# The filter's second product on the whole array, first loads behind the positions, and another order at the end of the prologue

## The chip, the cores and the metric

The kernel runs on one core of a Trainium2 chip. The metric is device time in microseconds of one execution, as the median of several runs. A profile of one execution shows each engine's instructions, the waits between engines and the DMA traffic: TensorE (PE, with its weight loads as PEld), VectorE (DVE), ScalarE (ACT), GpSimd (POOL) and SyncE (SP), which here only issues transfers.

## The reference

A long convolution is followed by a feed-forward block. For x and v of 4 x 12544 x 128 (batch, positions S, channels):

```
h_filt = (max(pos_emb @ w1, 0) @ w2) * exp(-0.01 * pos)
y      = irfft(rfft(x * v, 2S) * rfft(h_filt, 2S))[:S]
a      = x * y
out    = max(a @ m1, a @ m2, a @ m3) @ m_out
```

pos_emb is 12544 x 64, w1 64 x 64, w2 64 x 128; m1 to m3 are 128 x 768 and m_out is 768 x 128. All is float32 (the weights of the feed-forward block arrive as 64-bit floats and are converted on the chip).

## The kernel before, in words

The Fourier transforms are matrix products. A position is split in two indices, and a transform has a first stage over one (a table f1, 2 x 90 columns) and a second stage over the other, with twiddles folded into tables of weights `wt`; 45 pairs of frequencies (NK = 45, index g or s) are worked on one after the other. The inverse has a third stage per pair and a last stage per tile of output.

The instruction order on every engine is written out by hand: the program's order is each queue's order, and the framework only adds the waits that data, buffers and pools call for. A tile of a new pool that lies where a closed pool lay waits for the readers of that whole pool.

**Start.** TensorE runs products on zeros (`warm_up`), the window is transposed (`window_back`, lines 279 to 287), and `mlp_in` / `mlp_out` make the hidden layer of the filter from the positions (pos_emb, loaded in eight pieces over the queues of SP and ScalarE, line 266, into the space of `specH`). Behind the pieces SP issues the first raw weights (`load_raw`, line 177) and the first six units (`u_load`, line 325; a unit is 4 groups of x and v).

**First stages.** 16 quads for the filter (64 channels, into `specH`) and 32 units of batch 0 (into `spec`), with the conversion of the weights on VectorE between.

**Pair loop** (lines 805 to 839). Step s runs, for each pair, on TensorE:

- `s_second(s)`: the filter's second stage, from `specH` and `wt`, into the PSUM tile gps (line 770), copied by ScalarE to G (line 775). Each frequency has two sums, of which one needs the negated real part: `s_minus` makes it on GpSimd (`minus`, line 758). Each pair so has 8 products of 128 columns.
- `g_second(s)`: the second stage of batch 0 (`ps<-spec,wt`, line 130), evens copied by ScalarE to eo (line 161), butterfly on VectorE (lines 155 and 156).
- `s_filter(s - 1)`: the product with w2 (line 788), 16 products of 64 rows by 64 columns of weights with 128 columns of w2x, on four quarters of the array at a time, into sps (one buffer); ScalarE copies it to ht (line 793), and GpSimd issues ht's store to hd (line 796) for the later batches.
- `g_third(0, s - 3)`: the inverse's third stage of an earlier pair (`ps<-ab,wt`, line 130), copied to zs (line 440) and stored to zd from ScalarE's queue (line 446).

ScalarE's `g_swap` (lines 409 and 410) and VectorE's `g_re`, `g_im` and `g_unfold` (lines 415 to 427) multiply spectrum and filter of pair s - 2 and leave `ab`, which the third stage reads. Late in the loop, units of batch 1 are loaded, multiplied (line 332) and turned (line 337, two units at a time).

**Drain.** Steps 45 to 47 finish the last pairs; eight first-stage products of batch 1 (`u_first`, line 139, units 0 to 3) lie between the last third stages. Then come two turns, six folds of the weights (`fold`: a transpose pt by `eye` on line 750, its copy w1t, and pl, line 130), and the first stages of units 4 and 5. `pro` is closed, and its space goes to the pools of the main stage.

**Main stage.** 128 tiles in 4 batches. `t_load(b, i)` issues, on SP, two loads of zt from zd (line 495) and four of xT (line 502); `t_sums` and `t_last` make the tile's input gt (sums even and zt, product yps, gt on VectorE, line 528); `up` (pa, pb) and `down` (ops) are the feed-forward block. The convolution of the next batch runs beside it in slots.

## Time and profile before

| what | value |
|---|---|
| median of 5 runs | 2398.15 us (2394.39 to 2399.14) |
| profiled execution | 2400.21 us, span 2398.4 us |
| TensorE busy | 2365.5 us (99%) |
| TensorE weight loads | 1516.2 us (63%) |
| VectorE busy | 1317.2 us (55%) |
| ScalarE busy | 1018.1 us (42%) |
| GpSimd busy | 702.5 us (29%) |
| chain that ended last | TensorE 95%, then DMA, VectorE, ScalarE, GpSimd and issue with 1% each |

A busy TensorE is one with products in flight. Each float32 product appears as two records. In the profile's rows, "128*64 128x128" is a product on 128 rows and 64 columns of the array with 128 columns streamed; two such, on the two column halves, run side by side. The idle time in brackets behind a row is that of the engine before the row, with what ended it. PEclk is the clock granted to TensorE, as a share of full speed.

### The profile page before, as it was taken

The numbers are of one execution on the slowest core, as the hardware profiler recorded it, in microseconds if no ns is written. First come the engines' busy times: TensorE is split into PE (matmuls) and PEld (weight loads), VectorE is DVE, ScalarE is ACT, GpSimd is POOL, SyncE is SP. The second block draws the span as 40 slices with busy tenths as digits, with TensorE's granted clock in tenths as the row PEclk, the third lists the DMA queues.
The fourth block names the chain that finished last, engine by engine and source line by source line (L and its number), as shares of the span: only waits on it lengthen the run. The fifth ranks groups of instructions, "written<-read, shape, count | busy, mean of one in ns | idle before, by whom it ended". The sixth has DMA issues, their size and how long they took to land.

```text
span 2398.4 us, 67636 instructions
## 1 busy us (share of the span) xinstructions
PE 2365.5 (99%) x27853; PEld 1516.2 (63%) x27853; DVE 1317.2 (55%) x2806; ACT 1018.1 (42%) x1978; POOL 702.5 (29%) x775
## 2 busy tenths in 40 slices
PE   8999999999999999999999999999999999999998
PEld 7989856656555556666656556666655555666665
DVE  5578844466666645446666644446666643333333
ACT  2688844444444434444444424444444432222222
POOL 2045423222323211101111111101111105666666
PEclk9999999999999999999999999999999999999999
DMA  7778968767777659977777859967777742222221
GB/s 164 186 222 268 281 160 172 171 188 208 210 209 212 185 128 192 170 179 211 216 210 211 220 125 180 189 156 218 211 209 211 215 138 55 69 57 55 66 64 21
DMA packets 532221, 408.43 MB, mean 170 GB/s; under 512 B 375859, under 2 KB 421996, under 8 KB 531913
## 3 DMA queue, kind: packets, MB, share of 16 engines
q1 hardware_dynamic: 422240, 315.25, 53.3%
q10 hardware_dynamic: 100233, 67.88, 9.6%
q0 software_dynamic: 9440, 20.98, 3.6%
q8 instruction: 219, 3.59, 0.6%
q14 instruction: 89, 0.73, 0.1%
HBM read 295.69 MB, written 84.67 MB: 159 GB/s over the span
## 4 chain that ended last, share of the span: by engine, by line
PE 95%; DMA 1%; DVE 1%; ACT 1%; issue 1%; POOL 1%; ACTq 0%; SPq 0%; POOLq 0%; DVEq 0%
PE pb L130 21%; PE pa L130 21%; PE ops L130 18%; PE ps L130 12%; PE ps L139 7%; PE ops L601 5%; PE yps L130 5%; PE gps L770 1%; PE sps L788 1%; PE pm L299 1%; PE pst L337 1%; PE pw L130 1%; DMA zd<-zs 0%; DMA ut<-in_vr_dram 0%; POOL out_dram L625 0%
## 5 line engine op out<-in xcount | busy, mean ns | idle before, releaser
L541 DVE TENSOR_TENSOR hid<-hid,pb 128x392 f32<-128x392 f32 x768 | 431.4, 562 | 725.7 <-PE pb L130 494.3
L538 ACT ACTIVATE hid<-pa 128x392 f32<-128x392 f32 x768 | 381.5, 497 | 788.0 <-PE pa L130 614.9
L130 PE MATMUL pb<-gt,w_sb 128*64 128x392 f32 x3072 | 641.4, 493 | 4.9 <-ACT hid L538 4.8
L130 PE MATMUL pa<-gt,w_sb 128*64 128x392 f32 x3072 | 642.9, 494 | 0.8 <-DVE gt L528 0.8
L130 PE MATMUL ops<-hid,wo_sb 128*64 128x392 f32 x2304 | 481.2, 492 | 0.0
L420 POOL TENSOR_TENSOR xt<-xt,xs 128x512 f32<-128x512 f32 x135 | 172.2, 1276 | 890.2 <-DVE xs L419 657.0
L130 PEld LDWEIGHTS pb<-gt,w_sb 128*64 128x64 f32 x3072 | 227.5, 137 | 286.4 <-issue 250.6
L130 PEld LDWEIGHTS ops<-hid,wo_sb 128*64 128x64 f32 x2304 | 173.5, 137 | 205.8 <-issue 162.1
L130 PEld LDWEIGHTS pa<-gt,w_sb 128*64 128x64 f32 x3072 | 202.8, 137 | 60.8 <-issue 34.1
L139 PEld LDWEIGHTS ps<-f,uT 98*64 98x64 f32 x4096 | 178.6, 137 | 47.4 <-issue 43.7
L130 PEld LDWEIGHTS ps<-ab,wt 128*64 128x64 f32 x2880 | 166.1, 137 | 48.0 <-issue 30.9
L130 PEld LDWEIGHTS ps<-spec,wt 128*64 128x64 f32 x2880 | 172.2, 137 | 37.7 <-issue 34.8
L130 PE MATMUL ps<-spec,wt 128*64 128x128 f32 x2880 | 193.9, 273 | 1.4 <-issue 1.4
L130 PE MATMUL ps<-ab,wt 128*64 128x128 f32 x2880 | 191.4, 274 | 0.0
L352 POOL COPY planes<-ut 128x784 uint16<-128x784 uint16 x90 | 75.9, 844 | 389.3 <-DVE ut L332 294.9
L139 PE MATMUL ps<-f,uT 98*64 98x90 f32 x4096 | 188.9, 241 | 0.4 <-ACT zs L440 0.3
L445 DVE TENSOR_TENSOR zs<-ps,z 128x256 f32<-128x256 f32 x270 | 102.0, 419 | 97.0 <-ACT z L443 94.9
L130 PEld LDWEIGHTS yps<-f4p,zt 90*64 90x64 f32 x3584 | 134.4, 138 | 25.9 <-issue 22.6
L409 ACT ACTIVATE xs<-xt 64x512 f32<-64x512 f32 x180 | 113.2, 629 | 73.8 <-DVE xt L156 59.9
L427 DVE TENSOR_TENSOR ab<-xt 128x256 f32<-128x256 f32 x360 | 136.0, 419 | 4.5
L130 PE MATMUL yps<-f4p,zt 90*64 90x49 f32 x3584 | 137.7, 222 | 0.4 <-DVE zt L511 0.4
L528 DVE TENSOR_TENSOR gt<-yps,xT 128x392 f32<-128x392 f32 x128 | 72.5, 566 | 111.8 <-PE yps L130 67.6
(114 smaller groups left out, 2545.3 us busy)
## 6 DMA issues: line engine op xcount, KB each, us to landing
wt<-wt_const SPq DMA_DIRECT2D x360, 256.0 KB, 4.6
ht<-hd SPq DMA_DIRECT2D x270, 256.0 KB, 4.5
zd<-zs ACTq DMA_DIRECT2D x180, 256.0 KB, 4.6
zt<-zd SPq DMA_DIRECT2D x256, 180.0 KB, 3.9
ut<-in_xr_dram SPq DMA_DIRECT2D x128, 196.0 KB, 3.5
ut<-in_vr_dram SPq DMA_DIRECT2D x128, 196.0 KB, 4.0
xT<-in_x_dram SPq DMA_DIRECT2D x512, 49.0 KB, 2.7
out_dram<-ot ACTq DMA_DIRECT2D x96, 196.0 KB, 4.0
```

The costliest lines, as they stand in the source:

```text
L130: nc.tensor.matmul(out[64 * h:64 * h + 64], lhsT[:, 64 * h:64 * h + 64], rhs, start=start, stop=stop, skip_group_check=True)
L139: nc.tensor.matmul(ps[64 * c:64 * c + 64, 256 * i + r * N1:256 * i + (r + 1) * N1], a[:, r, :], table[:, c * N1:(c + 1) * N1], start=(i % ...
L299: nc.tensor.matmul(ps[64 * h:64 * h + HH, 512 * r + q * FO:512 * r + (q + 1) * FO], posv[64 * h:64 * h + 64, P - 1 - 2 * (8 * i + q) - r, ...
L352: nc.gpsimd.tensor_copy(pl_[:, :, :, 0:NB], a[:].bitcast(U16).rearrange("p s (n h) -> p h s n", h=2))
L409: nc.scalar.mul(xs[0:64], xt[64:128], -1.0)
L420: (nc.gpsimd if apart else nc.vector).tensor_tensor(out=xt[:], in0=xt[:], in1=xs[:], op=ALU.add)
L427: nc.vector.tensor_tensor(out=ab[:, :, q, :], in0=y[:, :, 0, :], in1=y[:, :, 1, :], op=op)
L445: nc.vector.tensor_tensor(out=zs[:, a], in0=ps[:, 0:256], in1=z1[:], op=op)
L528: nc.vector.tensor_tensor(out=g[:].rearrange("d p (m a) -> d p m a", a=2), in0=y, in1=xT[:].rearrange("d p (m a) -> d p m a", a=2), op=ALU ...
L538: nc.scalar.activation(h[:], pa[:, 0:N], Relu)
L541: nc.vector.tensor_tensor(out=h[:], in0=h[:], in1=pb[:, 0:N], op=ALU.max)
L601: nc.tensor.matmul(ps[64 * c:64 * c + 64, 0:H2], w, rhs[:, H2 * c:H2 * c + H2], start=start, stop=True, skip_group_check=True)
```

## The change

Four things change in the part before the main stage, and one in the order of its loads.

1. `s_second` makes 4 products in place of 8: the products with the real and the imaginary part of `specH` go to the two halves of gps and are not added up there. `s_minus` and its tile go.
2. `s_filter` adds them up: `w2x` holds w2 twice, with signs (`signs`, four scaled copies on ScalarE in place of one), and 8 products on 128 rows and 64 columns, with 256 columns streamed, take the place of the 16 quarter-array products. ht is copied from contiguous PSUM.
3. `g_third(0, s - 3)` and the load of its weights stand first in a step, ahead of `s_second(s)`, not behind `s_filter(s - 1)`.
4. The first raw weights and the first six units are issued from ScalarE's queue, behind `window_back`, and the last three warm-up products go. In the drain only units 0 and 1 have their first-stage products between third stages. Those of units 2, 3 and 4 stand one by one between the folds, alternating copies on ScalarE and VectorE, and those of unit 5 behind them.
5. `t_load` issues the four loads of xT ahead of the two of zt.

```
-    w2x = pin.tile([P, D], FP32, name="w2x")
+    w2x = pin.tile([P, 2, D], FP32, name="w2x")
...
-    def w2_order():
-        nc.scalar.copy(w2x[:].rearrange("f (c g) -> f c g", c=GC),
-                       w2_in[:].rearrange("f (g c) -> f c g", c=GC))
+    def signs():
+        for sg, lo_, m in ((0, 0, 1.0), (0, FO, 1.0), (1, 0, -1.0), (1, FO, 1.0)):
+            nc.scalar.mul(w2x[lo_:lo_ + FO, sg].rearrange("f (c g) -> f c g", c=GC),
+                          w2_in[lo_:lo_ + FO].rearrange("f (g c) -> f c g", c=GC), m)
...
     def t_load(b, i):
+        xT = hp.tile([D, 4, NB], FP32, tag="xT", name="xT", bufs=2)
+        for c in range(GC):
+            nc.sync.dma_start(xT[c * NG:(c + 1) * NG], x[:, 4 * i:4 * i + 4, c, b, :])
+        xTs[b, i] = xT
         zt = hp.tile([N1, 2, 512], FP32, tag="zt", name="zt", bufs=2)
...
-        xT = hp.tile([D, 4, NB], FP32, tag="xT", name="xT", bufs=2)
-        for c in range(GC):
-            nc.sync.dma_start(xT[c * NG:(c + 1) * NG], x[:, 4 * i:4 * i + 4, c, b, :])
-        xTs[b, i] = xT
...
     window_back()
-    warm_up(3)
-    raws.append(load_raw(*jobs[0], nc.sync))
-    u_load(0, 0)
-    u_load(0, 1)
-    raws.append(load_raw(*jobs[1], nc.sync))
+    raws.append(load_raw(*jobs[0], nc.scalar))
+    u_load(0, 0, nc.scalar)
+    u_load(0, 1, nc.scalar)
+    raws.append(load_raw(*jobs[1], nc.scalar))
     for u in range(2, 6):
-        u_load(0, u)
+        u_load(0, u, nc.scalar)
...
     def s_second(g):
         ps = gps.tile([P, 512], FP32, tag="g", name="gps")
-        m = minus.pop(g)
         for k in range(2):
             for r in range(2):
-                for q in range(2):
-                    lhsT = m[:, k] if q and r == 0 else specH[:, 2 * g + k, r, :]
-                    nc.tensor.matmul(ps[64 * q:64 * q + 64, k * P:(k + 1) * P],
-                                     lhsT, wf[g][:, k, r, :],
-                                     start=(k == 0 and r == 0), stop=True,
-                                     skip_group_check=True)
+                nc.tensor.matmul(ps[64 * r:64 * r + 64, k * P:(k + 1) * P],
+                                 specH[:, 2 * g + k, r, :], wf[g][:, k, r, :],
+                                 start=(k == 0), stop=True, skip_group_check=True)
...
     def s_filter(g):
-        for ri in range(2):
+        for c in range(2):
             for k in range(2):
-                for q in range(2):
-                    for h in range(2):
-                        at = 512 * q + (2 * ri + k) * D
-                        nc.tensor.matmul(
-                            ps[64 * h:64 * h + 64, at:at + D],
-                            G[64 * q:64 * q + 64, k, ri, :], w2x[64 * q:64 * q + 64],
-                            start=(ri == 0 and k == 0), stop=True, skip_group_check=True)
+                for h in range(2):
+                    nc.tensor.matmul(
+                        ps[64 * h:64 * h + 64, (2 * c + k) * 2 * D:(2 * c + k + 1) * 2 * D],
+                        G[:, k, c], w2x[:].rearrange("p s d -> p (s d)"), start=(k == 0),
+                        stop=True, skip_group_check=True)
...
     for s in range(NK + 3):
+        if s >= 3:
+            ws[s - 3, 1] = wi.pop(s - 3)
+            g_third(0, s - 3)
+            if s < NK:
+                wi[s] = load_dir(s, 1)
         if s < NK:
             ws[s, 0] = wf[s]
             s_second(s)
-            if s + 1 < NK:
-                s_minus(s + 1)
...
-        if s >= 3:
-            ws[s - 3, 1] = wi.pop(s - 3)
-            g_third(0, s - 3)
-            if s < NK:
-                wi[s] = load_dir(s, 1)
...
-        if NK <= s < NK + 2:
-            for v in range(4):
-                u_first(2 * (s - NK) + v // 2, v % 2, nc.scalar.copy)
-    folded = [fold(0)]
+        if s == NK:
+            for u in (0, 1):
+                for h in range(2):
+                    u_first(u, h, nc.scalar.copy)
     u_turn(4)
     u_turn(5)
-    for f in range(1, NF):
+    folded = []
+    for f in range(NF):
         folded.append(fold(f))
-        folded.pop(0)()
+        u_first(2 + f // 2, f % 2)
+        if f:
+            folded.pop(0)()
     folded.pop()()
     nc.scalar.copy(lin[:], pl[:, 0:D])
-    for u in (4, 5):
-        for h in range(2):
-            u_first(u, h)
+    for h in range(2):
+        u_first(5, h)
     pro.close()
```

## Prediction, made before the change was run

> **What bounds the kernel now.** I cut the span into its stages and read TensorE's busy time in each. Columns: stretch, its length, then busy time and instruction count of each engine, granted clock, DMA share, GB/s.
>
> ```profile
> 0.00:18.88 18.88, 14.14 (x103) 8.31 (x104) 2.24 (x4) 2.45 (x5) 4.72 (x12) 1.00 0.91 196
> 18.88:40.54 21.66, 20.07 (x513) 19.95 (x513) 10.57 (x17) 0.00 (x0) 0.00 (x0) 0.92 0.58 124
> 121.38:302.22 180.84, 175.72 (x3537) 157.92 (x3537) 154.29 (x311) 151.19 (x268) 88.33 (x130) 1.00 0.86 258
> 302.22:326.06 23.84, 18.88 (x343) 15.65 (x343) 8.72 (x16) 11.45 (x26) 4.82 (x7) 0.94 0.46 126
> 326.06:2398.40 2072.34, 2058.16 (x21696) 1240.73 (x21696) 1088.29 (x2330) 800.38 (x1616) 593.97 (x607) 1.00 0.65 163
> ```
>
> The last 2072 us, which the change leaves alone but for the order of loads issued two tiles ahead, are TensorE at over 99%. So whatever the change saves or costs before 326 us moves the end by as much. Three places count: the start, the pair loop (121 to 302) and the drain (302 to 326).
>
> At the start, the chain of waits:
>
> ```profile
> 14.29 1.45 PE pw L130 x12
> 15.73 3.15 issue
> 18.88 20.09 PE pm L299 x512
> ```
>
> The 3.15 us are the wait for the last piece of the positions. The DMA view of 0 to 18.9 us says what else had moved by then:
>
> ```profile
> DMA packets 1781, 3.71 MB, mean 196 GB/s; under 512 B 991, under 2 KB 1048, under 8 KB 1780
> ```
>
> In the pair loop one iteration takes 3.93 us (the quarter-tile products of L788 start at 187.76 and 191.69). TensorE's timeline, then ScalarE's and VectorE's (start, length, engine and line, tiles, count, idle time before and what ended it):
>
> ```profile
> 187.76 1.10 PE L788 MATMUL sps<-w2x,G 64*64 64x128 f32 x32
> 188.80 1.09 PE L130 MATMUL ps<-ab,wt 128*64 128x128 f32 x16
> 189.80 0.32 PE L770 MATMUL gps<-wt,minus 128*64 128x128 f32 x1
> ```
>
> ```profile
> 186.30 1.01 ACT L793 COPY ht<-sps 128x1024 f32<-128x1024 f32 x1
> 187.21 0.59 ACT L440 COPY zs<-ps 128x512 f32<-128x512 f32 x1
> 187.83 0.41 ACTq L446 DMA_DIRECT2D zd<-zs  x1
> 188.28 0.37 ACT L775 COPY G<-gps 128x256 f32<-128x256 f32 x1 [0.48 <-PE ps L130]
> ```
>
> ```profile
> 187.34 0.69 DVE L415 TENSOR_TENSOR xt<-xt,ht 128x512 f32<-128x512 f32 x1 [0.18 <-ACT ht L793]
> 189.47 0.76 DVE L427 TENSOR_TENSOR ab<-xt 128x256 f32<-128x256 f32 x2
> ```
>
> ScalarE goes from piece to piece with its own DMA issue in the only gap: it is full. VectorE starts L415 the moment ht is copied. TensorE is nearly full too. It is two limits at once, not one.
>
> In the drain, the chain again:
>
> ```profile
> 316.14 0.28 PE pt L750
> 316.42 0.02 SPq L495
> ...
> 317.62 4.29 DMA zt<-zd
> ```
>
> The load of the main stage's first zt is let go by **the last fold's transpose (pt)**, not by the last store of zs: that store was issued at 312.58. The new pool's tiles lie where the transposes' weights lay, and wait for their last reader. TensorE idles 3.05 us before the first yps.
>
> **The change, part by part.**
>
> *First loads held back.* By 18.88 us 3.71 MB had moved. Positions are 6 x 320 + 2 x 352 KB, constants and w1, w2, window about 410 KB: 3.1 MB. So 0.6 MB were raw weights and units ahead of the positions' tail. At 3.71 MB in about 17 us (0.218 MB/us) they cost 2.75 us. Their place is not wholly the positions' (SP's half had landed before ScalarE's half), so I take **-2.3 us**, bounds -0.8 and -2.75. The warm-up products that go (1.45 us) lie in the wait. The 20 issues now stand in ScalarE's queue behind winr's copy at 14.6 us; each waits for a free DMA slot. Behind them are only the scaled copies of w2: four of at most the 0.41 us of the one copy before, done before ScalarE's next work at 42 us. The loads ended at 31 us on SP; by the same bandwidth they end about there again, and nothing reads them before 40 us. If they came 10 us later, that cover would be gone.
>
> The granted clock was 0.50 from about 19.3 to 23 us: 86 products in 19 to 23 us against 34 per us after it, 1.47 us lost. The new gap is about 2.3 us; gaps of 1.6 us (at 39 us) kept the clock, gaps of 3.05 and 3.15 lost it. Between these I take half: **-0.7 us**, bounds 0 and -1.47.
> [...]
>
> *Fill of the pair loop.* The negated copy on GpSimd goes, and with it the one long wait for it, 0.90 us at 130.2 us, and a like wait of 0.4 at 121.8, which I leave in as ScalarE's G must now be the first in that pool. But the first third stage now stands ahead of the fourth second stage and waits for its VectorE chain. From the loop's start: two second stages of each kind end at 2.6 us, the first filter product at 4.5, its ht is copied by 5.6, VectorE ends at 8.2, 0.4 for that like wait: 8.6 us. The third filter product stands 2.2 us behind: 132.2 us against 133.03. **-0.9 us**, bounds -1.5 and 0.
>
> *One iteration, TensorE.* Paired 128-column products follow each other every 0.109 us (two per product pair). The filter's second stage falls from 8 to 4 such slots: -0.44. The filter with w2 had 32 records, four at a time, in 8 slots (1.03 with the change of tile shape). Now it has 16 records of 256 columns, two at a time: 8 slots of about 0.216, from the warm-up's 128x256 rows (12 records in 1.45 us, tail included): 1.72. That is +0.85. The two changes of shape go: each showed 0.2 us from start to start in place of 0.109 and a first product of 0.32 for 0.27, about 0.145; -0.29. The wait for minus (189.80 in place of 189.73, and the second column half late by one slot from there) goes: -0.13. Sum: 3.93 + 0.85 - 0.44 - 0.29 - 0.13 = 3.92 us.
>
> *One iteration, ScalarE.* The same copies of the same sizes in the same cyclic order: 3.93.
>
> *One iteration, the chain.* Third stage g now stands right behind filter g+1, not one iteration later. From a third stage's start: third 0.87, second of the filter 0.44, g_second 0.87, filter 1.72 with 0.17 tail, then ht 1.01, VectorE 2.6 to the first half of ab (187.34 to about 189.9), three handovers 0.15, half of the wait for ab's second half 0.1: 7.93 us, over two iterations: 3.97. Before there were three iterations for it, so it never bound. In TensorE's queue everything stands behind that wait, so it is late as a whole. Three limits of 3.92, 3.93 and 3.97 leave no slack: I take 3.97, bounds 3.92 and 4.10.
>
> From the third filter product to the last but one lie 41 iterations, which took 166.1 us (133.03 to 299.17). After: 41 x 3.97 = 162.8; six unit products on VectorE (0.56 each, of which 0.2 is slack): 2.1; two double transposes at 1.25 each, half of before (the second no longer waits 1.0 to 1.5 us for the butterfly, as its buffer is another): 2.5; DMA 0.8. Sum 168.2: **+2.1 us**, bounds -1 and +7.
>
> *Drain.* The last third stage comes some 2.7 us earlier and its store too, but that store isn't what is waited for. The last transpose now stands behind five first-stage products and the other folds. From the last-but-one filter product's start: its ht is copied at 2.9 us, the last filter product runs 3.0 to 4.9, its ht is ready at 6.3 (zs and two xs first), VectorE's ab at 8.95, the last third ends at 9.8, both turns at 11.0, the first fold's first-stage product (after uT's copy) at 12.3; four rounds of 1.25 (transpose 0.26, product 0.62, pl 0.22 and a change of shape) and the last transpose, 0.33: 17.7 us, against 17.2 before (316.4 - 299.17): +0.5, bounds -1.5 and +1. Behind it SP now issues the four xT first, for which the row is
>
> ```profile
> 319.55 1.97 SPq L502 DMA_DIRECT2D xT<-in_x_dram  x4
> ```
>
> so zt starts 2.0 us later, of which some 0.5 may come back in a shorter landing (4.3 for the first, 3.6 for the second tile). Behind it the second tile's loads come no later than before, as the number of issues is the same; at a batch's end xT no longer queues behind zt's wait for zd, which nobody waits for. TensorE is out of work at 320 either way; its wait grows from 3 to about 5 us. The half clock that follows is there already (0.50 from 324 to 330); the yps now meet it whole, +0.3. **+2.3 us**, bounds -0.5 and +3.5.
>
> **Sum**: -2.3 - 0.7 - 0.9 + 2.1 + 2.3 = +0.5 us. The profiled execution took 2400.21 us (span 2398.4), 2.06 above the median of the runs, 2398.15. It would be 2400.7; the median 2398.7.
>
> **The rivals.**
>
> *The drain works as it reads.* If xT and zt were let go by the last third stage's store instead, zt would land before the first-stage products end; 3.05 us of idle time and some 2.5 us of half clock would go: -5.5 in place of +2.3, in all -7.3: 2390.9 us. Against it: the chain goes from pt to SP. For it: nothing but that the order of memory may change with the pool.
>
> *The chain binds the pair loop* (the other side). If third waits for both halves of ab, and VectorE's and ScalarE's jitter adds up, an iteration is 4.10: 41 x 0.13 = +5.3 more, 2404.0 us. It decides from 4.08 us an iteration on (+4.5, in all +5.0). For it: L415 already starts 0.03 us after ht. Against: the first and second half of ab are waited for apart in the drain.
>
> *The positions come no sooner* (the first part does nothing): if ScalarE's own half of the positions is slow by itself, its last piece lands as before: +3.0, 2401.7 us.
>
> **How the numbers follow.** The forecast, no change that can be told, has 0.47; the drain that works 0.15; the chain 0.23; the late positions 0.11; 0.04 is for what I don't see. 0.2% is 4.8 us, about what a measurement of this kernel can tell from no change. Below 2393.4: the working drain and 0.01 of the rest, 0.16. Above 2402.9: the chain and 0.03 of the rest, 0.26. Within: the forecast and the late positions, 0.58. The sum's bounds together (-3.0 to +7 in the loop and drain) give 2393 to 2406; taken down to the working drain's upper half, 2391.5 to 2406.
>
> **What would show it.** Right: pm starts at about 16.6 us; quarter-tile products are gone and an iteration is 3.95 to 4.0 us with third stage waiting for VectorE's L427; pt ends about 17.7 us behind the last-but-one filter product, the four xT stand between it and zt, and TensorE idles about 5 us before yps. Wrong: pm at 18.8; an iteration at 4.1 or at 3.8; zt issued before the last fold's transpose.

## The result: 2403.3 us in place of 2400.6, and the profile after

The changed kernel took 2403.34 us (median of 26 runs, 2398.60 to 2406.42), the kernel before, run beside it, 2400.64 us (median of 50, 2394.39 to 2403.59). The ratio is 1.0012, 95% interval 1.0006 to 1.0017: 2.8 us slower, within the 0.2% that the prediction called no change, 2.3 us above its sum. The interval does not reach 1: the loss is small, but it is one.

The first profile of the changed kernel is that of its fastest run (2398.60 us), while the one of before was near its median. Comparing the two would show a gain of 1.6 us that the runs do not have. So a second execution, `after_again` (2405.46 us in the profiled run), is read beside it. "Half clock" below is a stretch in which the granted clock was 0.50. Length of each stage in us:

| stage | before | after | after_again |
|---|---|---|---|
| start, until the positions' products (pm) | 18.88 | 17.86 | 17.66 |
| pm | 20.07 | 19.87 | 20.18 |
| first stages | 82.43 | 81.22 | 82.22 |
| loop's start to the third filter product | 11.64 | 10.55 | 10.54 |
| 41 iterations, to the last but one | 166.14 | 165.59 | 165.65 |
| from there to the first yps | 23.61 | 25.13 | 25.39 |
| from there to the first pa | 26.88 | 28.35 | 28.61 |
| first pa to the end | 2072.3 | 2073.4 | 2078.3 |

The stretches of the changed kernel, with the columns of the table before (stretch, its length, busy time and count of PE, PEld, DVE, ACT, POOL, granted clock, DMA share, GB/s):

```profile
0.00:17.86 17.86, 13.41 (x92) 7.90 (x92) 2.24 (x4) 2.04 (x4) 4.72 (x12) 0.99 0.87 194
17.86:37.73 19.87, 19.86 (x512) 19.71 (x512) 9.02 (x14) 1.74 (x4) 0.00 (x0) 0.92 0.59 146
118.95:298.13 179.18, 177.77 (x2490) 147.66 (x2490) 154.25 (x311) 152.16 (x269) 45.17 (x86) 1.00 0.86 263
298.13:323.45 25.32, 18.34 (x311) 15.20 (x311) 9.61 (x18) 10.12 (x23) 5.08 (x8) 0.89 0.38 100
323.45:2396.80 2073.35, 2058.76 (x21696) 1240.90 (x21696) 1088.78 (x2330) 801.42 (x1616) 596.03 (x607) 1.00 0.66 163
```

The loop is 1.7 us shorter than its 180.84 us before, and GpSimd has 45 us of work there in place of 88 (no negated copies). The drain is 1.5 us longer with less TensorE work in it.

**Start.** The DMA view of the first 17.86 us, then the chain of waits:

```profile
DMA packets 1257, 3.47 MB, mean 194 GB/s; under 512 B 477, under 2 KB 534, under 8 KB 1257
```

```profile
15.28 2.57 issue
17.86 19.88 PE pm L302 x512
```

3.47 MB in place of 3.71. Of the 0.6 MB that were to be kept out, some 0.37 (3.47 less the 3.1 of positions and constants) still went ahead of the positions' end: ScalarE's queue is free for them from 15 us on.

**Loop.** TensorE's timeline:

```profile
189.35 1.90 PE L777 MATMUL sps<-w2x,G 128*64 128x256 f32 x16
191.07 1.05 PE L130 MATMUL ps<-ab,wt 128*64 128x128 f32 x16
191.95 0.61 PE L763 MATMUL gps<-wt,specH 128*64 128x128 f32 x8
192.39 1.04 PE L130 MATMUL ps<-spec,wt 128*64 128x128 f32 x16
193.26 1.90 PE L777 MATMUL sps<-w2x,G 128*64 128x256 f32 x16
```

This iteration is 3.91 us, with products behind each other without a wait; most of the 41 take 3.91 or 3.96. VectorE's timeline for the same pair shows how close the chain is:

```profile
192.34 0.69 DVE L418 TENSOR_TENSOR xt<-xt,ht 128x512 f32<-128x512 f32 x1 [0.29 <-ACT ht L782]
...
194.39 0.76 DVE L430 TENSOR_TENSOR ab<-xt 128x256 f32<-128x256 f32 x2
```

The first of the two halves of ab is done at about 194.8; the third stage that reads it starts at 194.99. There are 0.2 us of slack, so here TensorE sets the pace and not the chain over VectorE.

**Drain.** SP's queue, then what SP, VectorE and TensorE waited for:

```profile
313.03 1.76 SPq L498 DMA_DIRECT2D xT<-in_x_dram  x4
314.96 1.95 SPq L502 DMA_DIRECT2D zt<-zd  x2
```

```profile
SPq L498 <- PE pt L753: 18.6, 1, 18.6
```

```profile
319.43 0.69 DVE L513 TENSOR_TENSOR even<-zt 90x512 f32<-90x512 f32 x1 [3.45 <-DMA zt<-zd]
320.22 0.46 PE L130 MATMUL yps<-f4p,even 90*64 90x49 f32 x4 [4.82 <-DMA xT<-in_x_dram]
```

The last fold's transpose lets go xT, and zt stands behind four xT. VectorE waits for zt to make `even`, and the product yps reads `even`; the row of yps names xT, which is only what landed last before it. TensorE is idle for 4.82 us (5.08 in `after_again`) in place of 3.05.

### The profile page after: what moved, and what is told of

Same layout as the page of the kernel before. It is cut to its first block, busy times and chain, and to the rows that moved or that the text cites. A ratio compares the mean times of both kernels' runs of the same rounds, so it can differ in the third digit from the quotient of the medians.

```text
span 2396.8 us, 65298 instructions
## 1 busy us (share of the span) xinstructions
PE 2366.8 (99%) x26761; PEld 1505.1 (63%) x26761; DVE 1318.6 (55%) x2808; ACT 1020.2 (43%) x1979; POOL 661.1 (28%) x730
## 3 DMA queue, kind: packets, MB, share of 16 engines
q10 hardware_dynamic: 106953, 71.08, 10.2%
## 4 chain that ended last, share of the span: by engine, by line
PE 96%; DMA 1%; issue 1%; POOL 1%; ACT 1%; SPq 0%; DVE 0%; ACTq 0%; POOLq 0%; DVEq 0%
PE pb L130 21%; PE pa L130 21%; PE ops L130 18%; PE ps L130 13%; PE ps L139 8%; PE ops L604 5%; PE yps L130 5%; PE sps L777 3%; PE pm L302 1%; PE gps L763 1%; PE pst L340 1%; DMA specH<-in_pos_emb_dram 1%; POOL out_dram L628 0%; DMA hd<-ht 0%; ACT ht L782 0%
## 5 line engine op out<-in xcount | busy, mean ns | idle before, releaser
L130 PEld LDWEIGHTS ops<-hid,wo_sb 128*64 128x64 f32 x2304 | 173.5, 137 | 205.8 <-issue 164.5
L130 PEld LDWEIGHTS ps<-spec,wt 128*64 128x64 f32 x2880 | 167.9, 137 | 39.1 <-issue 34.5
L418 DVE TENSOR_TENSOR xt<-xt,ht 128x512 f32<-128x512 f32 x180 | 126.6, 703 | 15.3 <-ACT ht L782 15.0
```

Source lines behind the costliest of these rows:

```text
L130: nc.tensor.matmul(out[64 * h:64 * h + 64], lhsT[:, 64 * h:64 * h + 64], rhs, start=start, stop=stop, skip_group_check=True)
L418: nc.vector.tensor_tensor(out=xt[:], in0=xt[:], in1=hts[g][:, 0], op=ALU.mult)
```

## Experiments

All ratios are to the kernel before, run on the same chip beside each. The rows come from several chips, so ratios are to be compared and not medians; times "by the ratios" below are a difference of ratios times 2400 us.

| kernel | median us | ratio | 95% interval |
|---|---|---|---|
| first loads alone (loads_only) | 2401.86 | 1.0002 | 0.9994 to 1.0011 |
| whole-array filter alone (filter_only) | 2396.44 | 0.9980 | 0.9971 to 0.9989 |
| + third stage first (filter_third_first2) | 2396.24 | 0.9984 | 0.9976 to 0.9993 |
| + the new drain (filter_third_drain) | 2400.36 | 0.9995 | 0.9986 to 1.0004 |
| + first loads (after_zt_first2) | 2401.84 | 1.0004 | 0.9995 to 1.0013 |
| + xT ahead of zt = the change | 2403.34 | 1.0012 | 1.0006 to 1.0017 |
| the change again (after_again) | 2406.82 | 1.0022 | 1.0013 to 1.0031 |
| everything but the filter (order_only) | 2413.99 | 1.0054 | 1.0040 to 1.0067 |
| the change, two waits filled (after_warm2) | 2401.51 | 1.0004 | 0.9996 to 1.0013 |

From filter_only to the change each row adds one part. Neighbours' intervals overlap, so no single step is shown by the runs alone; the ends, 0.9980 and 1.0012, are clearly apart. From end to end the ratios lose 7.7 us. The profiles say where the steps lie.

### after_again: the changed kernel once more

No edit.

> The changed kernel as it is, profiled a second time, as its one profile had a span 1.6 us below that of the kernel before while its median lies 2.8 us above. Theory A (clock): TensorE's half clock comes in windows of 3.4 us whose place varies; the longer wait ahead of the first yps (4.8 us against 3.05) makes one window more fall on busy work in most executions. Then this profile shows the same length of the pair loop within 1 us and a longer stretch at half clock in the start or the drain, and a span of 2399 to 2404. Theory B (loop): the pair loop itself varies, its third stage waiting for VectorE more often; then 41 iterations take 168 us or more in place of 165.6. Time 2.5 to 3 us above before.

2406.82 us, higher than the first set. Up to the first pa it is 1.2 us ahead of before; behind it, 6.0 us are lost, in part to four waits for loads of weights (2.7 us in all, the longest 1.7 at 1924.8) and to a stretch at half clock of 6.8 us from 1980.5, behind the wait at the last batch's end, which is 2.64 us in before and 3.33 us here. In fourteen profiles this last part took 2072.3 to 2078.3 us: 2074.0 on average in the ten with zt issued ahead of xT, 2076.4 in the four with xT first. Theory A, one more stretch at half clock in the start or the drain, is not what this profile shows: the extra stretch lies at the last batch's end, and the loop is the same to 0.1 us.

### loads_only, filter_only, order_only: the parts alone

loads_only:
```
-    warm_up(3)
-    raws.append(load_raw(*jobs[0], nc.sync))
+    raws.append(load_raw(*jobs[0], nc.scalar))
...
-        u_load(0, u)
+        u_load(0, u, nc.scalar)
```


> Of the change only the first loads behind window_back and the three warm-up products less. Forecast's account: the first product of the positions at 17.9 us (as in the changed kernel's profile) and not 18.9, and the time 1 to 3 us below before. Rival (positions no sooner, or clock and TensorE's earlier start cost what the loads give): within 0.5 us of before.

No change, as its rival had it. pm starts 1.1 us sooner (17.81), but now TensorE waits on without warm-up products, half clock lies over 6.8 us from 15.3 on, and pm takes 20.42 us.

filter_only (parts 1 and 2 of the change; loop order, drain, loads as before):
```
-                for q in range(2):
-                    lhsT = m[:, k] if q and r == 0 else specH[:, 2 * g + k, r, :]
...
+                nc.tensor.matmul(ps[64 * r:64 * r + 64, k * P:(k + 1) * P],
+                                 specH[:, 2 * g + k, r, :], wf[g][:, k, r, :],
...
+                        G[:, k, c], w2x[:].rearrange("p s d -> p (s d)"), start=(k == 0),
```


> Of the change only the filter's second stage in 4 products and the product with w2 on the whole array; the third stage stays behind the filter's product, the drain and the loads stay as before. Forecast's account: an iteration is bound by ScalarE at 3.93 and by TensorE at 3.92, the 0.13 us waits for minus are gone, so 41 iterations take 163 to 167 us against 166.1, and the time is -2 to +1 us of before, as the recovery at 3.80 after a disturbance is lost. Rival (the quarter tiles were worth more): 168 us or more and +2 to +5 us.

0.2% faster, more than the 2 us that were expected at most. The third filter product comes 8.77 us after the loop's start in place of 11.64 (1.3 us of this are two waits ahead of products that read the negated copies, 0.42 and 0.90 us; the profile names `minus` for the longer one); the 41 iterations take 165.35 us (-0.8), the drain 0.7 us less: 4.4 us in all, against 4.8 by the runs. (The 41 iterations vary by about 1 us: in loads_only, whose loop is that of before, they took 167.23 us against 166.14.)

order_only (third stage first, the new drain, xT first; filter and loads as before):
```
     for s in range(NK + 3):
+        if s >= 3:
+            ws[s - 3, 1] = wi.pop(s - 3)
+            g_third(0, s - 3)
```


> Of the change only the order: third stage first in a step, first-stage products between the folds, xT ahead of zt; quarter-array filter and early loads as before. Forecast's account: the drain costs 2 us (fold's last transpose as late as before, zt 2 us behind it, TensorE idle some 5 us ahead of yps), and the loop gains or loses under 2 us, so +1 to +4 us. Rival (the order is what helps): the main stage's first pa starts earlier behind the last-but-one filter product than the 26.9 us of before, and the time is below before.

13 us slower, which neither account had. The 41 iterations take 171.70 us. What TensorE's third stage waits for in the loop, here and then in the changed kernel (us in total, times, longest):

```profile
PE ps L130 <- DVE ab L427: 7.9, 18, 1.3
```

```profile
PE ps L130 <- DVE ab L430: 1.0, 2, 0.6
```

The longest wait of each row still lies ahead of the third filter product. With the quarter-array filter TensorE comes to the third stage before ab is there, every second iteration, though its own products take no longer. ScalarE's timeline of order_only shows why ht, and so ab, is late:

```profile
200.13 0.37 ACT L161 COPY eo<-ps 128x256 f32<-128x256 f32 x1 [0.35 <-PE ps L130]
201.80 1.01 ACT L793 COPY ht<-sps 128x1024 f32<-128x1024 f32 x1
```

The filter product ended at 201.11, but ScalarE copies eo and then xs twice (1.67 us) first, and can begin only when the second stage of batch 0 is done. Under the 1.03 us of the quarter-array product these copies do not fit, and ht comes 0.69 us late. In the changed kernel they lie under the whole-array product of 1.73 us, and ht's copy starts 0.04 us behind it (191.25, 191.29). So the new order is nearly free only with the whole-array filter; that it is the product's length, and not the shorter second stage ahead of it, is read from these rows, and no run takes the two apart. It is a chain that binds, as in the prediction's second rival, but in another kernel and with ScalarE's copies in it.

### filter_third_first2 and filter_third_drain: one step each

filter_third_first2 is filter_only with the edit shown last. filter_third_drain adds:
```
-        if NK <= s < NK + 2:
-            for v in range(4):
-                u_first(2 * (s - NK) + v // 2, v % 2, nc.scalar.copy)
...
+        folded.append(fold(f))
+        u_first(2 + f // 2, f % 2)
```


> The whole-array filter alone (which took 2396.4), plus the third stage ahead of the second stages in each step; loads, drain and t_load as before the change. Theory A (with the whole-array filter the third stage's place costs nothing in the loop, as TensorE's filter product is long enough): 41 iterations 165.4 to 165.8 us as with the filter alone (165.35); the third filter product 10.5 us after the loop's start in place of 8.8 (the first third stage is waited for): +1.7; the last third stage comes sooner in the drain, but the first zt is let go by the last fold's transpose as ever: 0 to -1; in all 2397 to 2399. Theory B (the chain from ht to the third stage binds): 41 iterations 168 us or more, 2400 to 2404. Theory C (the place of the third stage is what turns the filter's gain into a loss, by more waits in the main stage): 2402 to 2406.

> The whole-array filter with the third stage first (2396.24, ratio 0.9984), plus the change's drain: first-stage products of units 2 to 4 between the folds. First loads and t_load as before the change. Theory A (the drain's new order costs by itself, since the last fold's transpose, which lets the first zt go, stands behind five more first-stage products): the last transpose ends 17.85 us after the last-but-one filter product in place of 16.2, yps 23.2 to 23.6 in place of 21.5, first pa 26.5 to 26.9 in place of 24.1: +2.7 us, and with TensorE's wait of 3 us in place of 2.0 often one half-clock window more: 2398.5 to 2401, ratio 0.9995 to 1.0005. Theory B (the first loads and their half-clock windows made the difference between 2396 and 2402): the drain costs 0 to 1 us, 2396 to 2397.5.

Third stage first: 164.18 us for the 41 iterations, 10.54 us to the third filter product (+1.8: the first third stage must be waited for, and stands ahead of one more pair of second stages), and 2.1 us less in the drain (last transpose 16.18 us, first pa 24.08 us after the last-but-one filter product). 0.87 us of both is only where the count begins: one third stage more lies ahead of the third filter product, and one fewer behind the last but one. That leaves +0.9 and -1.2, and the runs show no difference: theory A, but for a drain that gained more than the 0 to 1 us that it allowed. The new drain: last transpose 17.84, yps 23.60, first pa 26.38: +2.3 us, at the place that theory A named, and +2.6 us by the ratios, whose intervals overlap. What SP waits for, behind a wait for the last store of zs, is the transpose:

```profile
SPq L498 <- PE pt L753: 4.9, 1, 4.9
```

### after_zt_first2: only the order of xT and zt undone

```
-        xT = hp.tile([D, 4, NB], FP32, tag="xT", name="xT", bufs=2)
...
         zts[b, i] = zt[:, 0], zt[:, 1]
+        xT = hp.tile([D, 4, NB], FP32, tag="xT", name="xT", bufs=2)
```


> The changed kernel with one thing undone: t_load issues zt ahead of xT again. Theory A (the drain pays for four xT issues, nothing else does): the first zt is issued 2.0 us sooner, 17.9 us after the last-but-one filter product in place of 19.9; yps 23.1 in place of 25.1 to 25.4; TensorE's wait ahead of yps 3 us in place of 4.8 to 5.1, the half-clock window 6.8 us in place of up to 10.2; main stage unchanged: 2.5 to 3.5 us less than the changed kernel (2403.3 to 2406.8), so 2401 to 2403, a ratio to before of 1.000. Theory B (the order of xT and zt also costs time in the main stage, at the batch ends, where loads for the next batch stand behind each other; the three profiles with xT first took 2073.4, 2078.3 and 2078.0 us from the first pa on, those with zt first 2072.3, 2073.1 and 2075.7): 3 us more go there, in all 6 us less, 2398 to 2400, ratio 0.998 to 0.999. Theory C (the new order of the third stage costs it all): no change, 2403 to 2407.

zt is issued 17.92 us after the last-but-one filter product in place of 19.86, TensorE waits 3.29 us in place of 4.82 to 5.08, first pa 26.82 in place of 28.35 to 28.61: 1.5 to 1.8 us. The ratios give 1.9 (against the change) to 4.3 (against after_again). The intervals of both pairs overlap. Theory A is what the rows show up to the first pa; whether B adds something in the main stage the runs cannot tell. The averages of the last part above (2.4 us more with xT first) point to B, but single profiles of one order differ by up to 4.9 us.

### after_warm2: products that nobody reads in two waits

```
     window_back()
+    warm_up(6)
...
+    pw = cps.tile([P, 512], FP32, tag="cv", name="pwd")
+    for _ in range(18):
+        halves_mm(pw[:, 0:P], f1[:, 0:P], f1[:, 0:P], True, True)
     pro.close()
```


> The changed kernel with products that nobody reads in two of TensorE's waits: 6 pairs of products on zeros behind the window (2.9 us, in the wait for the positions) and 18 pairs of 128 columns behind the last first-stage product (3.9 us, in the wait for the first zt). Theory A (the half-clock windows that follow these waits come from the idle time and cost what they seem to): no half clock from 17.5 to 24 us and none from 318 to 328 us; the product over the positions takes 18.3 to 18.5 us in place of 19.9 to 20.2, and the first pa comes 2.5 to 4 us sooner after the last filter products (24.5 to 26 us in place of 28.4 to 28.6 after the last-but-one filter product): 4 to 5.5 us less, 2399 to 2402, and a mean granted clock of 0.997 to 0.998 in place of 0.994 to 0.996. Theory B (the clock follows something else, such as the change of work): windows of half clock stay where they are, and the time is 2403 to 2408.

At the start theory A holds: the wait ahead of pm falls from 2.86 to 1.05 us, the clock stays at 1.00, and pm takes 19.01 us, if not 18.3 to 18.5. The same two stretches of the changed kernel and then of this one:

```profile
19.00:23.00 4.00, 4.00 (x100) 4.00 (x98) 1.29 (x2) 0.00 (x0) 0.00 (x0) 0.76 0.87 224
```

```profile
19.00:23.00 4.00, 4.00 (x117) 4.00 (x115) 1.53 (x3) 0.00 (x0) 0.00 (x0) 1.00 1.18 258
```

In the drain it mostly fails: the wait falls to 1.05 us, yet half clock comes at 322.4 for 3.4 us, behind the broken row of yps, and the first pa is only 0.6 to 0.8 us sooner. The rows show 1.4 to 2.0 us up to the first pa. By the ratios it is 2 to 4 us, with intervals that overlap, so that more than the rows' part is gained is not shown. Another stretch at half clock came at 39.1 us, behind the wait of 1.58 us ahead of the first stages. The granted clock, averaged over an execution, was 0.995 or less in 14 of 26 executions of the change and 5 of 11 of after_again, in 5 of 11 of loads_only and 8 of 11 of after_zt_first2; in 4 of 27 and 4 of 35 of before, in 3 of 12 of filter_third_drain and of filter_fold_first2 and 2 of 5 of order_only, in none of 22 of the two kernels filter_only and filter_third_first2, in none of 11 here, and in none of 21 of the three kernels best0 to best2 below, which have the six pairs too. The executions with the lower clock are the longer ones (2404.6 us mean at 0.994 against 2402.3 at 0.996, of the change).

### filter_fold_first2 and best0: the folds elsewhere

filter_fold_first2 puts all six folds behind the last filter product, with filter_only for the rest:
```
+        if s == NK:
+            folded = []
+            for f in range(NF):
+                folded.append(fold(f))
+                if f:
+                    folded.pop(0)()
```


> The whole-array filter alone, plus another drain: all six folds (transposes, copies, products) directly behind the last filter product, while the third stage's chain runs; then the last two third stages, then the two turns and all twelve first-stage products of batch 1. Loads, loop and t_load as before the change. Theory A (the first zt waits for the last reader of the closed pool, the last fold's transpose; with the folds out of the way it waits for the last third stage's store only): the first zt is issued 14 to 15 us after the last-but-one filter product in place of 17.35, lands under the first-stage products; TensorE's wait ahead of yps goes from 2.3 us to under 1, and the half-clock window of 6.8 us there with it: yps 19.5 to 20.5 us after the last-but-one filter product in place of 22.9, first pa 3 to 6 us sooner in all, 2391 to 2394, ratio 0.995 to 0.997. Theory B (zt waits for the last store of zs, or for the readers in another way, whatever the folds do): zt issued at 17 us or later, no gain, 2396 to 2398.

0.9987 (0.9979 to 0.9996), no better than the filter alone: theory A fell. The transposes end at 10.06 us after the last-but-one filter product, but zt is issued at 17.80. What SP waits for, and three rows of TensorE's timeline:

```profile
SPq L498 <- DMA zd<-zs: 13.6, 2, 12.6
```

```profile
300.35 0.44 PE L130 MATMUL pl<-wo_sb,w1t 128*64 128x128 f32 x4 [1.22 <-ACT w1t L755]
...
303.88 3.04 PE L130 MATMUL ps<-ab,wt 128*64 128x128 f32 x32
...
317.57 0.32 PE L130 MATMUL yps<-f4p,even 90*64 90x49 f32 x4 [1.80 <-DMA f4p<-f4p_const]
```

The wait moved three times: the fold's copies w1t stood behind ht and zs on ScalarE, so the folds took 5.4 us; the third stages stood behind the folds and so the store of zs came late; and the load of f4p stood behind ScalarE's copies of the first stages.

best0 was to mend this (third stage, then folds, then first-stage products; f4p loaded at the start; six pairs of warm-up products at the start; third stage behind the filter in the loop, as before the change; zt first):
```
+        if s >= NK:
+            ws[s - 3, 1] = wi.pop(s - 3)
+            g_third(0, s - 3)
...
+            u_turn(4)
+            u_turn(5)
+    folded = []
+    for f in range(NF):
+        folded.append(fold(f))
...
+    for u in range(2, 6):
```


> A kernel made of what paid. From the change: the whole-array filter and the first loads on ScalarE's queue. Other than the change: six pairs of warm-up products stand in the wait for the positions; the third stage stays behind the filter product in the loop and goes first only in the last three steps; the last third stage comes directly behind the first-stage products of units 0 and 1 and the turns, the folds behind it, all other first-stage products at the end; f4p is loaded at the start; zt ahead of xT. Expected if zt waits for the later of the last fold's transpose and the last store of zs: last third stage ends some 10 us after the last-but-one filter product, store landed and last transpose done at 13.5, zt issued at 13.5 to 14.5, yps at 19 to 20.5 in place of 22.9 with the filter alone, TensorE's wait under 1.5 us and no half clock there: first pa 3 to 5 us sooner than with the filter alone by the drain, 2 us by the start (no half clock there): 2389 to 2393, ratio 0.995 to 0.9965. If the wait only moves (the folds' transposes late behind ScalarE's copies, or SP late by the xT of the tile before): 2394 to 2396.

2395.27 us, 0.9977 (0.9967 to 0.9986): the case in which the wait moves. Three stretches of 4 us around its folds (304.1 to 310.7):

```profile
303.00:307.00 4.00, 2.50 (x33) 1.66 (x29) 0.00 (x0) 1.77 (x5) 0.00 (x0) 1.00 0.39 132
307.00:311.00 4.00, 4.00 (x30) 2.44 (x29) 0.00 (x0) 1.17 (x5) 1.35 (x2) 0.50 0.02 5
311.00:315.00 4.00, 4.00 (x72) 4.00 (x72) 1.07 (x2) 0.66 (x2) 1.38 (x2) 0.65 0.55 142
```

After a wait of 1.50 us and the first folds the clock is at half for 6.8 us; TensorE then needs all of its time for 30 products in 4 us. filter_fold_first2, with a wait of 1.22 us among its folds, lost it too (at 302.8). The folds in a row of before and of best1, with no wait longer than 0.2 us among them, kept it, and so did those between first-stage products, in the change. So among folds the clock was lost in the two kernels with a wait of 1.50 or 1.22 us and thin work behind it, and kept in the kernels without such a wait; a row of folds by itself did not lose it here.

### best1 and best2: another drain, and the first loads on either queue

best1 is best0 with another drain, best2 is best1 with the first loads on SP as before the change:
```
+        if NK <= s < NK + 2:
+            for u in ((0, 1), (2,))[s - NK]:
+                for h in range(2):
+                    u_first(u, h, nc.scalar.copy)
+    folded = [fold(0)]
...
+    for u in (3, 4, 5):
+        for h in range(2):
+            u_first(u, h, copies[1 - h])
```


> The kernel best0 (2395.27) with another drain: the third stage first only in the last three steps, first-stage products of units 0 and 1 in the first of them and of unit 2 in the second, then the turns and folds as before the change, then the first-stage products of units 3 to 5. First loads on ScalarE's queue and six pairs of warm-up products as in best0. Expected if the first zt waits only for the last fold's transpose: that ends 15.0 to 15.3 us after the last-but-one filter product (16.2 with the third stage first and the old drain, less two products of 0.62), yps at 20.3 to 21, TensorE's wait ahead of them 0.8 to 1.3 us, no half clock there or one window; third filter product 8.8 us after the loop's start; no half clock over the positions: 2390 to 2393, ratio 0.9955 to 0.997. If folds in a row lose the clock by themselves, as in best0 (half clock from 307.0 on behind a wait of 1.5 us): 2394 to 2396.

> As best1, but with the first raw weights and units on SP's queue ahead of ScalarE's half of the positions' tail, as before the change (with the six pairs of warm-up products). Theory A (holding the first loads back brings the positions 0.7 to 1.0 us sooner, and this shows once the half clock over them is gone): product over the positions starts 0.7 to 1.0 us later than in best1, no half clock either way; time 0.5 to 1 us above best1. Theory B (what the positions gain the first stages lose, by raw weights and units that come later or DMA that is busy anyway): the same as best1 or below it.

best1: 2391.19 us (5 runs, 2388.73 to 2395.34), 0.9962 (0.9949 to 0.9976); best2: 2393.09 us, 0.9972 (0.9960 to 0.9983). Both are faster than before and than the change. They are not told apart from each other by time, nor is best1 from the filter alone (0.9971 to 0.9989). Start and drain of best1:

```profile
18.13:37.14 19.01, 19.01 (x512) 18.86 (x512) 9.02 (x14) 1.75 (x4) 0.00 (x0) 1.00 0.70 154
...
295.05:316.23 21.18, 18.17 (x323) 14.75 (x319) 9.22 (x17) 10.97 (x25) 4.82 (x7) 1.00 0.51 138
```

pm at full clock, and a drain with 0.93 us of wait ahead of yps and no half clock until 316.9, just behind the first pa, where 3.4 us of it follow all the same. The last transpose came at 16.00 us, not 15.0 to 15.3: with the third stage behind the filter in the loop, one third stage more (0.87 us) lies behind the last-but-one filter product than in filter_third_first2, from which that number was worked out. In best2 pm starts 0.8 us later, as its theory A had it, but half clock comes at 20.1 us behind a wait of only 1.58 us, so pm takes 20.08 us. The row of pm in best2, and that of filter_third_first2, in which a longer wait lost nothing:

```profile
18.90 20.08 PE L304 MATMUL pm<-w_sb,specH 64*41 64x64 f32 x512 [1.58 <-issue]
18.14 19.02 PE L302 MATMUL pm<-w_sb,specH 64*41 64x64 f32 x512 [1.83 <-issue]
```

## Why the prediction was right in its total, and where its terms were not

The total, +0.5 us for no change that can be told, was measured as +2.8. The drain's mechanism and the fill were read rightly from the trace. Of the signs named for being right, those of the drain came (pt, four xT ahead of zt, 5 us of idle time); pm at 16.6 us and a third stage that waits for VectorE did not. The other terms were mis-sized in both directions, and that the total still fell within no change is in part luck: in the two profiles the terms of the sum come to -1.4 and -1.0 us, the first stages, which the prediction left out, to -1.2 and -0.2 (81.0 to 83.7 us over fourteen profiles), and the last part to +1.1 and +6.0.

- **First loads held back, -2.3 us: too much.** The rows show -1.0 and -1.2; over seven profiles with the loads held back pm starts at 17.90 us on average, over seven without at 18.63: -0.7, just short of the small end of the bounds (-0.8). The step that failed took all 0.6 MB as kept out of the way. The held-back loads start at 15 us, as the queue of ScalarE is free then, and 0.37 MB of them still share the DMA engines with the positions' tail. That this sharing is the whole reason is argued from the bytes; no run holds them back further.
- **Clock at the start, -0.7 us: wrong.** pm takes 19.87 and 20.18 us against 20.07. The wait is not 2.3 us but 2.86 and 4.20. The 2.3 us were the old wait with the warm-up products' 1.45 us added and 2.3 us of earlier positions taken off; with 1.0 to 1.2 us in place of 2.3 it comes to about 3.5, and the window's products, behind which the wait begins, ended 0.7 us later and 0.8 us earlier than before. Half the clock is lost as before, in some executions for longer (6.8 us in loads_only and after_zt_first2). One stretch of 3.4 us at half clock over pm cost 1.05 us (20.07 less 19.02), not 1.47: that compared with 34 products per us, a rate that pm does not keep (512 in 19.02 us are 27 per us). With six pairs of products in the wait, three profiles of four lost no clock (19.01 to 19.02 us), best2 did. The prediction let the warm-up products go as lying in the wait; more of them there was what saved time.
- **Fill, -0.9 us: right** (-1.1). The filter alone gives -2.9, and the third stage first takes 1.8 of it back. The wait of 0.4 us that was left in did not come.
- **Loop, +2.1 us: mis-sized by 2.6** (-0.5). The limit was TensorE, forecast at 3.92, and not the chain over VectorE: iterations of 3.91 and 3.96 us take turns, and the third stage waits in one of the 41 alone (0.48 us at 163.38; the other of the two waits counted beside order_only's, 0.57 us, is in the fill), as the chain's term of 2.6 us from ht to the first half of ab measures 2.5 (192.34 to about 194.8), and the half wait for ab's second half was not paid. That is some 1.3 us of the 2.6. The units' products were to cost 2.1 us; the iterations with them in the loop take some 0.6 us more than their neighbours. The turns cost 1.2 us each, as forecast.
- **Drain, +2.3 us: right in mechanism, 0.6 to 0.8 too high.** The last transpose ended 17.85 us after the last-but-one filter product (forecast 17.7), the four xT stood ahead of zt (issued at 19.86, 2.5 us later than before), TensorE waited 4.82 and 5.08 us (forecast: about 5). The first yps came 1.5 to 1.8 us later; zt to yps took 5.3 us in place of 6.3, 1.0 of the 2.0 us came back where 0.5 was allowed.
- **The rest, 0: wrong.** With these terms and the first stages the first pa comes 1.2 to 2.6 us sooner than before, yet the kernel is 2.8 us slower. The step that failed is the one that carried whatever happens before 326 us to the end unchanged: the last part took 1.1 and 6.0 us more. In the profiles it varies by 6 us, with waits for weights and with the half clock at the last batch's end; the runs' mean clock says that the change has more half clock. The kernels without warm-up products in the start's wait have it most often (32 of 59 executions of the change, after_again, loads_only and after_zt_first2); that is a count and no experiment: the 1.4 to 2.0 us that filling two waits took off lie ahead of the first pa. Against filter_only, the first pa comes 2.4 and 3.9 us later, of the 7.7 us by the ratios. The rest must lie in the last part, but the profile of filter_only, with 2075.7 us there, does not show it. How much of it is the order of xT and zt in the main stage stays open.

Of the rivals, the drain that works as it reads did not come about: zt waited for pt, as the chain had said, 4.9 us behind the store in filter_third_drain, and filter_fold_first2 shows that its cure is not just to move the folds. The chain that binds did not come about either, but a chain of its kind is real: order_only has 171.70 us for the 41 iterations. That the rival's sum was 173.5 (168.2 + 5.3), close by, is chance: it was worked out for the changed kernel. The positions did come sooner, by less.

The stretches at half clock that end within a profile last 3.4, 6.8 or 10.2 us here (3.4 over pm and 6.8 in the drain in before, 3.4 and 10.2 in the changed kernel). Waits that lost the clock and waits that kept it are not told apart by their length: those of 1.58 us (best2, ahead of pm) and 1.50 us (best0, with thin folds behind it) lost the clock, while one of 1.83 us (filter_third_first2, ahead of pm) and those of 2.64 and 2.71 us at the last batch's end (before, until 1979 us, and the changed kernel, until 1978 us) kept it. The wait of 1.58 us ahead of the first stages (it ends at 38 to 41 us), the same in thirteen profiles, lost the clock in three (after_zt_first2, after_warm2, best2) and kept it in ten. So the half that the forecast took for a wait of 2.3 us, between gaps of 1.6 and of 3.05 and 3.15 us in one profile, was no more than the author's estimate; what decides whether a wait loses the clock these runs do not show.

Whether the transposes in the folds have a part in the lost clock of best0 is not shown either: the same transposes in a row in before and best1 kept it, and no run here takes them alone.

## What to carry to other kernels

When a change moves loads behind a queue's other work, ask when that queue falls free: the loads were held back only until then (15 us here). Products that nobody reads, in a wait for data, are not waste to be removed with the change: enough of them to leave a wait of about 1 us (1.05 in after_warm2) held the clock at 1.00 here (19.01 us for pm in place of 19.9 to 20.7). When a wait for a pool's last reader ends a stage, list every later link (the stores behind third stages, copies on the same queue, small loads) before the readers are moved; the wait went to each of them in turn here, and a version with the whole-array filter, the first loads held back, warm-up products in the wait, the third stage first in the last three steps alone and two first-stage products moved (best1) gained 0.4%, where the whole reorder lost the filter's gain.

## What was not expected of the hardware

- Half clock came behind waits of 1.50 us (best0) and 1.58 us (best2), and not behind one of 1.83 us (filter_third_first2) or of 2.64 us (before). The same wait of 1.58 us in the same place lost the clock in three profiles and kept it in ten, so neither length nor place alone decided it here.
- The longer whole-array product (16 records of 256 columns, 1.73 us, against 32 of 128 on quarters, 1.03 us) made the kernel faster (0.9980 alone): with it go half of the second stage's products and the negated copies with their waits, and with the third stage first ScalarE's copies fit under it.
- One profile misleads by more than the effect: the last 2070 us, the same instructions in all kernels but for some loads, took from 2072.3 to 2078.3 us.
